# Transposing the late attention chunks by DMA, with a new load order at the start, in a retention-plus-FFN kernel

## Chip, cores, metric

The kernel runs on one core of a Trainium2 chip (trn2). The metric is device time in microseconds (us) of one execution; the quoted times are medians of repeated executions, and the profile is one further execution.

## The reference, cut to what matters

```python
# q, k, v: (B=4, H=8, S=768, D=64), fp32
for t in range(S):
    state = gamma * state + outer(k[t], v[t])        # one 64x64 state per head
    y[t] = scale * (q[t] @ state)
x = y.transpose(0, 2, 1, 3).reshape(3072, 512)
h = maximum(x @ w_in, 0)                             # w_in 512 x 2048   ("FFN1")
out = (h * h) @ w_out                                # w_out 2048 x 512  ("FFN2")
```

The kernel cuts the sequence into 24 chunks of 128 tokens with all eight heads. A chunk's attention is a *visit* on TensorE: scores and state sums of one chunk, and values and state application of the chunk before. It needs k and q with the head dimension on the partitions, that is transposed; this transposition is what the change is about. Each chunk then passes FFN1 and FFN2.

## The kernel before

The kernel is a list of operations with estimated durations. A small list scheduler in the program places them and so fixes the instruction order of every engine and of the DMA issues on SyncE's queue (SP). The hardware then runs each engine's list in order, waiting on semaphores. The estimates don't make the kernel fast or slow by themselves, but they decide what stands behind what.

```python
SMALL = (1.20, 1.55, 65)      # a 256 KB load of one chunk's k, q or v: 256-byte runs
PAIR  = (1.4, 1.6, 9)         # a 512 KB load of k or q of two chunks: long runs
BLOCKS = [1, 1, 2, 2, 2, 4, 4, 4, 4]     # chunks of one FFN1 pass
LEAD = 7                      # attention visits this many chunks ahead of the FFN
ORDER = "p0 i0 i1 p1 i2 i3 o0 o1 o2 p2 o3"   # p: pair of chunks, i: quarter of w_in, o: of w_out
...
    def flips(m):             # transposition in the visit: 32 TensorE transposes of 64x64
        for x, name in enumerate("kq"):
            for j in range(NJ):
                for sub in range(2):
                    r = slice(L * sub, L * sub + L)
                    for a in range(2):
                        nc.tensor.transpose(tpv[...], bf[name][m % NBF][r, j, a, :], ident[r, r])
    def evacuate(m):          # PSUM -> SBUF on ScalarE
        pl.add(f"E{m}", "ACT", 1.0, ("yy0", "yy1"), qkeys(m), lambda: nc.scalar.activation(...))
...
        def fn():             # one visit
            if t is not None: flips(t)
            if m is not None: values(m); apply(m, 0); ...
            if n is not None: scores(n); sums(n)
            if m is not None: ...; apply(m, 1)
```

The first six chunks are loaded in pairs and transposed by another TensorE routine (`flip_rows`, left out here), the other 18 by `flips`, one chunk ahead.

Of the kernel before, what the change touches and what calls it, by code (L numbers as in the profile page):

```python
# [18 lines left out]
class Plan:  # L19
# [44 lines left out]
    def schedule(self, nbanks, max_open):  # L64
# [21 lines left out]
        shared = [0.0, 0.0]  # L86
# [3 lines left out]
        while done < n:  # L90
# [25 lines left out]
            if move:  # L116
                out_ = outstanding[eng]
                while out_ and out_[0][0] <= t:
                    out_.pop(0)
                while sum(x[1] for x in out_) + dur[2] > self.RING:  # L120
                    t = max(t, out_.pop(0)[0])
# [8 lines left out]
            if move:  # L130
                dur, n_desc = (dur[:2] if t < 50 else dur[:1] * 2), dur[2]
                eng_free[eng] = t + 0.08
                for w in range(2):
                    shared[w] = max(shared[w], t + self.DMA_LATENCY) + dur[w]
                end[i] = max(shared) + self.LAND
                out_.append((max(shared), n_desc))
                dur = 0.08
            else:
                if eng == "PE":
# [6 lines left out]
                    while issued + todo > edge:  # L146
# [7 lines left out]
                        next_fetched = ahead + min(5.7, max(0.3, max(shared) - ahead)) + self.FETCH  # L154
# [23 lines left out]
SMALL = (1.20, 1.55, 65)  # L178
PAIR = (1.4, 1.6, 9)
WIDE = (2.75, 2.75, 33)  # L180
STORE = (0.72, 0.72, 9)
BLOCKS = [1, 1, 2, 2, 2, 4, 4, 4, 4]
SPLIT = 6
WARM = 20.0
FILL = 0.8
PACE = 6
LEAD = 7
NFP = 3
F2LAG = 5.0
# [7 lines left out]
ORDER = "p0 i0 i1 p1 i2 i3 o0 o1 o2 p2 o3"  # L197


def dma_order(nm):  # L200

    seq = []
    for t in ORDER.split() + [f"c{m}" for m in range(nm)]:
        n = int(t[1:])
        if t[0] == "p":
            new = [("k", 2 * n), ("q", 2 * n), ("v", 2 * n), ("v", 2 * n + 1)]
        else:
            new = [(x, n) for x in "kqv"] if t[0] == "c" else [("in" if t[0] == "i" else "out", n)]
        seq += [x for x in new if x not in seq]
    return seq  # L210
# [3 lines left out]
def kernel(  # L214
# [32 lines left out]
    NLD, NBF, NQT, NXT, NH2, NWS, NOSB, NST = 4, 4, 4, 4, 3, 4, 3, 6  # L247
# [18 lines left out]
    bf = {x: [sb(f"{x}s{j}", [P, NJ, 2, D] if x != "v" else [P, H, D], BF16) for j in range(NBF)] for x in "qkv"}  # L266
# [81 lines left out]
    def prepare(m):  # L348
        b, i = where(m)
        slot = m % NLD  # L350
        for x in "kqv":
            t = ld[x][:, slot, :]
            if x != "v" and m < 2 * NFP:
                if m % 2 == 0:
                    pl.add(f"ld{x}{m}", "SP", PAIR, (), (f"ld{x}{slot}", f"ld{x}{slot + 1}"),
                           lambda x=x: nc.sync.dma_start(  # L356
                               ld[x][:, slot : slot + 2, :].rearrange("s u n -> s (u n)"),
                               src[x][b, :, i * C : (i + 2) * C, :].rearrange("h (w t) d -> w h (t d)", t=16)),
                           prio=dma_prio[(x, m)])
                continue  # L360
            pl.add(f"ld{x}{m}", "SP", SMALL, (), (f"ld{x}{slot}",),
                   lambda x=x, t=t: nc.sync.dma_start(  # L362
                       t.rearrange("s (h d) -> s h d", h=H),
                       src[x][b, :, i * C : (i + 1) * C, :].rearrange("h s d -> s h d")),
                   prio=dma_prio[(x, m)])
        for x in "kq":
            t, o = ld[x][:, slot, :], bf[x][m % NBF]
            if m < 2 * NFP:
                pl.add(f"c{x}{m}", CAST[x], 0, (f"ld{x}{slot}",), (f"bf{x}{m % NBF}",),
                       lambda on, t=t, o=o: copy_on(on, o.rearrange("s j a d -> s (j a d)"), t), prio=urgency(m))  # L370
                continue
# [8 lines left out]
               prio=urgency(m))  # L380

# [10 lines left out]
    def flip_rows(m, x):  # L392


        to, key = (sc, "sc") if x == "k" else (yy, "yy")
        for u in range(2):
            bt = bf[x][(m + u) % NBF].rearrange("s j a d -> s (j a d)")

            def fn(u=u, bt=bt):
                for t in range(8):  # L400
                    for a in range(2):
                        nc.tensor.matmul(to[L * a : L * a + L, u, L * t : L * t + L], lhsT=bt[:, t * D : t * D + D],  # L402
                                         rhs=ident.rearrange("p (w h) -> p w h", h=H)[:, :, NJ * a : NJ * a + NJ],
                                         start=True, stop=True, skip_group_check=True)
            pl.add(f"T{x}{m}.{u}", "PE", 0.35, (f"bf{x}{(m + u) % NBF}", "ident"), (f"{key}{u}",), fn,
                   prio=-200 + m, lat=0.2, count=16)
        cols = to.rearrange("p s n -> p (s n)").rearrange("p (t u w j) -> p u j w t", u=2, j=NJ, w=8)
        for u in range(2):
            o = qkts[(m + u) % NQT][:, "kq".index(x)].rearrange("p j (w t) -> p j w t", t=16)
            pl.add(f"E{x}{m + u}", EVAC, 0, (f"{key}0", f"{key}1"), (f"qkT{(m + u) % NQT}.{x}",),  # L410
                   lambda on, u=u, o=o: copy_on(on, o, cols[:, u]), prio=urgency(m + u), lat=0.05)

    def natural_keys(m):

# [15 lines left out]
    def qkeys(m):  # L430
        return [f"qkT{m % NQT}.{x}" for x in "kq"]
# [295 lines left out]
```

## Time and profile before

| | before |
|---|---|
| median | 226.32 us (225.99 to 226.65, 3 runs) |
| profiled span | 225.5 us |
| TensorE (PE) busy | 204.8 us, 91% |
| all FFN at full rate | 24 x 8 x 0.865 = 166 us (four 128x512 matmuls take 0.865 us) |

The table of windows of the kernel before follows. Its columns are: stretch in us and its length; busy us (with instruction count) of PE, PEld (weight loads), VectorE (DVE), ScalarE (ACT), GpSimd (POOL); granted TensorE clock (1.00 is full speed); DMA share (mean busy share of the 16 DMA engines; it can pass 1, because packets overlap and each is counted where it starts); GB/s.

```profile
24.00:30.00 6.00, 4.41 (x145) 3.90 (x143) 5.54 (x12) 3.86 (x8) 1.36 (x3) 1.00 1.03 364
36.00:42.00 6.00, 3.44 (x59) 2.87 (x57) 3.39 (x8) 2.61 (x6) 1.64 (x2) 1.00 1.05 190
42.00:48.00 6.00, 5.52 (x102) 4.12 (x102) 5.33 (x12) 3.55 (x7) 0.88 (x2) 1.00 0.94 300
48.00:60.00 12.00, 11.71 (x213) 5.80 (x215) 4.25 (x8) 5.01 (x8) 4.91 (x8) 1.00 1.03 245
96.00:108.00 12.00, 11.89 (x312) 6.27 (x315) 11.74 (x25) 8.82 (x14) 3.65 (x6) 1.00 0.89 193
```

Before 48 us DMA is full (share about 1) and PE has gaps; after it PE is nearly full. Weights move at some 360 GB/s, the small loads at 190 to 200. A second view is the chain of waits of before, start and length in us: TensorE's progress hangs on DMA until 42 us, above all on the queries of the third pair.

```profile
10.01 6.26 SPq L362
16.31 5.24 SPq L569
25.69 16.56 DMA qn<-in_q_dram
42.37 0.81 POOL qs L345
```

The third view is the timeline of TensorE in one visit of before: start, length, line, tiles. L389 is `flips`.

```profile
98.38 0.32 PE L389 MATMUL yy<-ident,ks 64*64 64x64 bf16 x16
98.53 0.30 PE L389 MATMUL yy<-ident,qs 64*64 64x64 bf16 x16
98.65 0.30 PE L453 MATMUL yy<-pt,vs 64*64 64x64 bf16 x16
98.78 0.24 PE L468 MATMUL yy<-qkT,state 64*64 64x64 bf16 x8
98.84 0.31 PE L479 MATMUL sc<-qkT 64*64 64x64 bf16 x16
98.97 0.32 PE L490 MATMUL sc<-vs,ks 64*64 64x64 bf16 x16
99.11 0.27 PE L468 MATMUL yy<-qkT,state 64*64 64x64 bf16 x8
99.31 0.39 PE L593 MATMUL fps<-xt,w_in 128*128 128x512 bf16 x1
```

Matmuls are pipelined, so one reads from start to start: the flips hold TensorE from 98.38 to 98.65, 0.27 us, of a visit of 0.93 us.

### The profile page before, as it was taken

How to read it: one execution, taken by the hardware profiler on the slowest of the kernel's cores; microseconds unless marked ns; L12 is line 12 of the kernel's file. 1: busy time of each engine (PE TensorE's matmuls, PEld its weight loads, DVE VectorE, ACT ScalarE, POOL GpSimd, SP SyncE). 2: the span in 40 equal slices, each digit the busy share in tenths (PEclk: the TensorE clock that was granted, in tenths of full speed). 3: DMA queues.
4: the chain of work that ended last, by engine and by line, in shares of the span. 5: the costliest groups of instructions: out<-in, count | busy, mean ns of one | idle time of the engine just before them, and what ended most of it. 6: DMA issues, size and time to landing. Idle time of an engine off the chain costs nothing.

```text
span 225.5 us, 7244 instructions
## 1 busy us (share of the span) xinstructions
PE 204.8 (91%) x3210; PEld 116.0 (51%) x3236; DVE 112.7 (50%) x250; ACT 106.0 (47%) x168; POOL 39.0 (17%) x65
## 2 busy tenths in 40 slices
PE   4786778699999999999989999999999999999993
PEld 1545667554577875455545554444444444444441
DVE  1583955873188786699957765432222222220000
ACT  8315635644357552677555555434335444343121
POOL 3213224224323322332242200000000000000000
PEclk9997999999999999999999999999999999999999
DMA  6999999999999999998988510110011110111212
GB/s 150 265 337 189 337 376 237 184 346 197 283 211 200 236 187 213 231 202 179 206 188 177 146 49 3 47 49 12 35 47 47 49 47 1 47 49 47 93 49 91
DMA packets 70975, 34.02 MB, mean 151 GB/s; under 512 B 63008, under 2 KB 63008, under 8 KB 70944
## 3 DMA queue, kind: packets, MB, share of 16 engines
q1 hardware_dynamic: 70944, 33.56, 58.8%
q8 instruction: 25, 0.41, 0.8%
q14 instruction: 6, 0.05, 0.1%
HBM read 27.26 MB, written 6.29 MB: 149 GB/s over the span
## 4 chain that ended last, share of the span: by engine, by line
PE 75%; SPq 11%; DMA 7%; issue 2%; ACT 2%; DVE 1%; POOL 0%; ACTq 0%; POOLq 0%
PE fps L631 34%; PE fps L593 32%; DMA qn<-in_q_dram 7%; SPq L569 6%; SPq L362 4%; PE yy L389 3%; PE yy L468 2%; SPq L356 2%; PE yy L453 1%; ACT qkT L436 1%; PE sc L479 1%; PE sc L490 1%; DVE xt L555 1%; POOL qs L345 0%; PE yy L402 0%
## 5 line engine op out<-in xcount | busy, mean ns | idle before, releaser
L593 PE MATMUL fps<-xt,w_in 128*128 128x512 bf16 (+2 forms) x566 | 93.7, 309 | 3.9 <-POOL w_in L345 2.0
L631 PE MATMUL fps<-w_out,h 128*128 128x512 bf16 x368 | 90.1, 379 | 1.7 <-issue 1.3
L598 ACT ACTIVATE h<-fps 128x512 bf16<-128x512 f32 x96 | 56.6, 596 | 52.6 <-PE fps L593 51.5
L593 PEld LDWEIGHTS <-w_in 128*128 128x128 bf16 x576 | 50.5, 99 | 35.4 <-issue 2.1
L603 DVE TENSOR_TENSOR h<-h 128x512 bf16<-128x512 bf16 x96 | 42.4, 456 | 49.7 <-ACT h L598 49.5
L631 PEld LDWEIGHTS <-h 128*128 128x128 bf16 x384 | 36.7, 98 | 42.9
L555 DVE TENSOR_TENSOR xt<-yy,yf 128x512 bf16<-128x512 f32 x24 | 16.6, 690 | 21.6 <-ACT qkT L436 18.1
L436 ACT ACTIVATE qkT<-yy 128x1024 bf16<-128x1024 bf16 x18 | 18.4, 1023 | 18.2 <-PE yy L468 17.5
L639 ACT ACTIVATE osb<-fps 128x512 f32<-128x512 f32 x24 | 14.3, 597 | 21.7 <-PE fps L631 21.4
L377 DVE TENSOR_TENSOR vs<-vn,vf 128x512 bf16<-128x512 f32 x24 | 17.6, 735 | 4.8 <-DMA vn<-in_v_dram 4.8
L345 POOL CAST ks<-kn 128x512 bf16<-128x512 f32 x20 | 13.5, 677 | 35.0 <-DMA kn<-in_k_dram 19.8
L345 POOL CAST qs<-qn 128x512 bf16<-128x512 f32 x21 | 14.7, 701 | 27.3 <-DMA qn<-in_q_dram 27.3
L546 DVE TENSOR_TENSOR state<-sc,state 128x256 bf16<-128x256 f32 x40 | 16.7, 419 | 0.5
L533 DVE TENSOR_TENSOR pt<-sc,cmask 128x512 bf16<-128x512 f32 x24 | 16.3, 681 | 0.0
L468 PE MATMUL yy<-qkT,state 64*64 64x64 bf16 x352 | 12.5, 198 | 1.0 <-issue 0.6
L453 PE MATMUL yy<-pt,vs 64*64 64x64 bf16 x384 | 7.8, 195 | 2.8 <-DVE pt L533 1.4
L468 PEld LDWEIGHTS <-state 64*64 64x64 bf16 x352 | 7.6, 105 | 2.0 <-PE yy L468 1.1
L453 PEld LDWEIGHTS <-vs 64*64 64x64 bf16 x384 | 5.3, 107 | 5.5 <-issue 2.9
L479 PE MATMUL sc<-qkT 64*64 64x64 bf16 x384 | 7.9, 196 | 0.1
L341 ACT ACTIVATE w_in<-wst 128x512 bf16<-128x512 f32 x7 | 4.1, 623 | 7.7 <-DMA wst<-in_moe_w_in_dram 7.6
L490 PE MATMUL sc<-vs,ks 64*64 64x64 bf16 x352 | 7.6, 196 | 0.0
L693 PE MATMUL fps<-ident 128*128 128x512 bf16 x12 | 5.8, 605 | 1.6 <-POOL ident L297 1.6
(45 smaller groups left out, 85.0 us busy)
## 6 DMA issues: line engine op xcount, KB each, us to landing
vn<-in_v_dram SPq DMA_DIRECT2D x24, 256.0 KB, 5.9
out_dram<-osb SPq DMA_DIRECT2D x24, 256.0 KB, 2.0
kn<-in_k_dram SPq DMA_DIRECT2D x18, 256.0 KB, 5.5
qn<-in_q_dram SPq DMA_DIRECT2D x18, 256.0 KB, 5.7
wst<-in_moe_w_in_dram SPq DMA_DIRECT2D x4, 1024.0 KB, 9.7
wst<-in_moe_w_out_dram SPq DMA_DIRECT2D x4, 1024.0 KB, 10.5
kn<-in_k_dram SPq DMA_DIRECT2D x3, 512.0 KB, 11.6
qn<-in_q_dram SPq DMA_DIRECT2D x3, 512.0 KB, 13.4
```

What stands on the lines that cost most here:

```text
L345: nc.gpsimd.tensor_copy(o, t)
L377: lambda: nc.vector.tensor_tensor(out=o[:], in0=t.rearrange("s (h d) -> s h d", h=H), in1=vf[:, i, :, None].to_broadcast([P, H, D]), op=AL ...
L436: lambda: nc.scalar.activation(qkT.rearrange("p x j (s t) -> p s (x j) t", s=2), tpv.rearrange("p s (g t) -> p s g t", t=L), AF.Copy), pri ...
L453: nc.tensor.matmul(yy[L * c : L * c + L, sub, p * L : p * L + L], lhsT=vs[r, 4 * a + j, :], rhs=pt[r, a, j, :], start=(p == 0), stop=True, ...
L468: nc.tensor.matmul(yy[L * c : L * c + L, sub, p * L : p * L + L], lhsT=st[r, j, :], rhs=qkT[r, 1, j, sub * L : sub * L + L], start=False, ...
L533: lambda: nc.vector.tensor_tensor(out=pt[:], in0=sc[:, :, 0:256].rearrange("s g (p t) -> s g p t", p=NJ), in1=cmask[:, None, None, :].to_b ...
L546: f = lambda cc=cc, j1=j1, j0=j0: nc.vector.tensor_tensor(out=sts[j1][:], in0=cc, in1=sts[j0][:], op=ALU.add)
L555: lambda: nc.vector.tensor_tensor(out=xt[:, :, u * C : u * C + C].rearrange("s p (g t) -> s g p t", g=2), in0=yy[:, :, 0:256].rearrange("s ...
L593: nc.tensor.matmul(ps[:, u * n : u * n + n], lhsT=w_in_bf[j][:, cb, c * P : (c + 1) * P], rhs=xt[:, cb, cols], start=(cb == 0), stop=(cb = ...
L598: nc.scalar.activation(h2[:, f0 : f0 + per, cols], ps[:].rearrange("p (u n) -> p u n", u=per), AF.Relu)
L603: nc.vector.tensor_mul(hv, hv, hv)
L631: nc.tensor.matmul(ps[:], lhsT=h2[:, fb, u * C : u * C + C], rhs=w_out_bf[j][:, c, :], start=(fb == 0), stop=(fb == NFB - 1))
```

## The change

The intent: from the ninth chunk on, let the DMA transpose k and q, four chunks ahead, so that TensorE and ScalarE are rid of it; and at the start fetch four chunks before the weights, so that their attention is done while TensorE would be idle. Single-chunk loads replace the pairs; the first four queries are issued on ScalarE's queue; FFN1 starts with six single chunks; the last chunk's FFN2 is cut into two halves.

```diff
-BLOCKS = [1, 1, 2, 2, 2, 4, 4, 4, 4]
+BLOCKS = [1, 1, 1, 1, 1, 1, 2, 2, 2, 4, 4, 4]
+AHEAD = 4
-LEAD = 7
+LEAD = 2
+NPE = 6      # chunks 0-5: eight 128x128 TensorE transposes each, outside the visit
+NTD = 8      # chunks 6, 7: flips in the visit; from 8 on: DMA
+QACT = 4
-F2LAG = 5.0
+F2LAG = 3.0
-ORDER = "p0 i0 i1 p1 i2 i3 o0 o1 o2 p2 o3"
+ORDER = ("k0 q0 q1 v0 k1 q2 v1 k2 v2 v3 k3 q3 i0 i1 q4 o0 i2 i3 k4 o1 v4 o2 o3 v5 v6 q5 k5 q6 v7 q7 k6 k7")
...
+            side = x == "q" and m < QACT
+            pl.add(f"ld{x}{m}", "ACT" if side else "SP", SMALL, (), (f"ld{x}{slot}",), ...
...
+        if m >= NPE:
+            pl.add(f"X{m}", "SP", TURN, (f"bfk{m % NBF}", f"bfq{m % NBF}"), qkeys(m),
+                   lambda: nc.sync.dma_start_transpose(out=qkT..., in_=t...), prio=-0.5)
...
+            parts = 2 if q4 == NM - 1 else 1      # FFN2 of the last chunk in halves
+                    ... prio=(q4 + F2LAG) * 8 + 2 * j + 1 + part * 0.5
```

(`flip_rows` and its helpers go; buffers of the bf16 and transposed k/q grow from 4 to 5; the scheduler's model of DMA is simplified and its estimates for DMAs are changed; PACE, the number of first visits that go ahead of everything else, grows from 6 to 8.)

More of the change, by code (lines that the diff above doesn't have):

```diff
@@ L85, in schedule @@
         open_groups = set()
-        shared = [0.0, 0.0]
+        pipe = 0.0
         outstanding = {e: [] for e in eng_free}
@@ L116, in schedule @@
             if move:
+                cost, n_desc, hold = dur
                 out_ = outstanding[eng]
@@ L119, in schedule @@
                     out_.pop(0)
-                while sum(x[1] for x in out_) + dur[2] > self.RING:
+                while sum(x[1] for x in out_) + n_desc > self.RING:
                     t = max(t, out_.pop(0)[0])
@@ L130, in schedule @@
             if move:
-                dur, n_desc = (dur[:2] if t < 50 else dur[:1] * 2), dur[2]
-                eng_free[eng] = t + 0.08
-                for w in range(2):
-                    shared[w] = max(shared[w], t + self.DMA_LATENCY) + dur[w]
-                end[i] = max(shared) + self.LAND
-                out_.append((max(shared), n_desc))
-                dur = 0.08
+                eng_free[eng] = t + hold
+                pipe = max(pipe, t + self.DMA_LATENCY) + cost
+                end[i] = pipe + self.LAND
+                out_.append((pipe, n_desc))
+                dur = hold
             else:
@@ L153, in schedule @@
                         edge += self.BLOCK
-                        next_fetched = ahead + min(5.7, max(0.3, max(shared) - ahead)) + self.FETCH
+                        next_fetched = ahead + min(5.7, max(0.3, pipe - ahead)) + self.FETCH
                     issued += todo
@@ L175, in schedule @@
         return sorted(range(n), key=lambda i: (start[i], i))
-SMALL = (1.20, 1.55, 65)
-PAIR = (1.4, 1.6, 9)
-WIDE = (2.75, 2.75, 33)
-STORE = (0.72, 0.72, 9)
-BLOCKS = [1, 1, 2, 2, 2, 4, 4, 4, 4]
+SMALL = (1.20, 65, 0.6)
+TURN = (1.10, 16, 2.4)
+WIDE = (2.85, 33, 0.6)
+STORE = (0.80, 9, 0.6)
+BLOCKS = [1, 1, 1, 1, 1, 1, 2, 2, 2, 4, 4, 4]
 SPLIT = 6
+AHEAD = 4
 WARM = 20.0
 FILL = 0.8
-PACE = 6
-LEAD = 7
-NFP = 3
-F2LAG = 5.0
+PACE = 8
+LEAD = 2
[3 more added lines that the diff above has]
+F2LAG = 3.0
 F2WAIT = 4
@@ L194 @@
 WPRIO = {"in": -2.0, "out": 2.0}
-ORDER = "p0 i0 i1 p1 i2 i3 o0 o1 o2 p2 o3"
+ORDER = (
+    "k0 q0 q1 v0 k1 q2 v1 k2 v2 v3 k3 q3 i0 i1 q4 o0 i2 i3 k4 o1 v4 o2 o3 v5 v6 q5 k5 q6 v7 q7 k6 k7"
+)
 def dma_order(nm):
-    seq = []
-    for t in ORDER.split() + [f"c{m}" for m in range(nm)]:
-        n = int(t[1:])
-        if t[0] == "p":
-            new = [("k", 2 * n), ("q", 2 * n), ("v", 2 * n), ("v", 2 * n + 1)]
-        else:
-            new = [(x, n) for x in "kqv"] if t[0] == "c" else [("in" if t[0] == "i" else "out", n)]
-        seq += [x for x in new if x not in seq]
-    return seq
+    names = {"i": "in", "o": "out"}
+    seq = [(names.get(t[0], t[0]), int(t[1:])) for t in ORDER.split()]
+    return seq + [(x, m) for m in range(nm) for x in "kqv" if (x, m) not in seq]
 @with_exitstack
@@ L246 @@
         assert 512 % (n * C) == 0 and x // 4 == (x + n - 1) // 4
-    NLD, NBF, NQT, NXT, NH2, NWS, NOSB, NST = 4, 4, 4, 4, 3, 4, 3, 6
+    NLD, NBF, NQT, NXT, NH2, NWS, NOSB, NST = 4, 5, 5, 4, 3, 4, 3, 6
     NBANK = 4
@@ L265 @@
     ld = {x: sb(f"{x}n", [P, NLD, H * D], FP32) for x in "qkv"}
-    bf = {x: [sb(f"{x}s{j}", [P, NJ, 2, D] if x != "v" else [P, H, D], BF16) for j in range(NBF)] for x in "qkv"}
+    kq = [sb(f"kqs{j}", [P, 2, NJ, 2, D], BF16) for j in range(NBF)]
+    bf = {"k": [t[:, 0] for t in kq], "q": [t[:, 1] for t in kq]}
+    bf["v"] = [sb(f"vs{j}", [P, H, D], BF16) for j in range(NBF)]
     qkts = [sb(f"qkT{j}", [P, 2, NJ, P], BF16) for j in range(NQT)]
@@ L352, in prepare @@
             t = ld[x][:, slot, :]
-            if x != "v" and m < 2 * NFP:
-                if m % 2 == 0:
-                    pl.add(f"ld{x}{m}", "SP", PAIR, (), (f"ld{x}{slot}", f"ld{x}{slot + 1}"),
-                           lambda x=x: nc.sync.dma_start(
-                               ld[x][:, slot : slot + 2, :].rearrange("s u n -> s (u n)"),
-                               src[x][b, :, i * C : (i + 2) * C, :].rearrange("h (w t) d -> w h (t d)", t=16)),
-                           prio=dma_prio[(x, m)])
-                continue
-            pl.add(f"ld{x}{m}", "SP", SMALL, (), (f"ld{x}{slot}",),
-                   lambda x=x, t=t: nc.sync.dma_start(
+            side = x == "q" and m < QACT
+            pl.add(f"ld{x}{m}", "ACT" if side else "SP", SMALL, (), (f"ld{x}{slot}",),
+                   lambda x=x, t=t, q_=nc.scalar if side else nc.sync: q_.dma_start(
                        t.rearrange("s (h d) -> s h d", h=H),
                        src[x][b, :, i * C : (i + 1) * C, :].rearrange("h s d -> s h d")),
-                   prio=dma_prio[(x, m)])
+                   prio=dma_prio[(x, m)] - 200 * side)
         for x in "kq":
             t, o = ld[x][:, slot, :], bf[x][m % NBF]
-            if m < 2 * NFP:
-                pl.add(f"c{x}{m}", CAST[x], 0, (f"ld{x}{slot}",), (f"bf{x}{m % NBF}",),
-                       lambda on, t=t, o=o: copy_on(on, o.rearrange("s j a d -> s (j a d)"), t), prio=urgency(m))
-                continue
             pl.add(f"c{x}{m}", CAST[x], 0, (f"ld{x}{slot}",), (f"bf{x}{m % NBF}",),
@@ L380, in prepare, with qkeys @@
                prio=urgency(m))
+    def qkeys(m):
+        return [f"qkT{m % NQT}.{x}" for x in "kq"]
     def flips(m):
@@ L390, in flips @@
                                             bf[name][m % NBF][r, j, a, :], ident[r, r])
-    def flip_rows(m, x):
-        to, key = (sc, "sc") if x == "k" else (yy, "yy")
-        for u in range(2):
-            bt = bf[x][(m + u) % NBF].rearrange("s j a d -> s (j a d)")
-            def fn(u=u, bt=bt):
-                for t in range(8):
-                    for a in range(2):
-                        nc.tensor.matmul(to[L * a : L * a + L, u, L * t : L * t + L], lhsT=bt[:, t * D : t * D + D],
-                                         rhs=ident.rearrange("p (w h) -> p w h", h=H)[:, :, NJ * a : NJ * a + NJ],
-                                         start=True, stop=True, skip_group_check=True)
-            pl.add(f"T{x}{m}.{u}", "PE", 0.35, (f"bf{x}{(m + u) % NBF}", "ident"), (f"{key}{u}",), fn,
-                   prio=-200 + m, lat=0.2, count=16)
-        cols = to.rearrange("p s n -> p (s n)").rearrange("p (t u w j) -> p u j w t", u=2, j=NJ, w=8)
-        for u in range(2):
-            o = qkts[(m + u) % NQT][:, "kq".index(x)].rearrange("p j (w t) -> p j w t", t=16)
-            pl.add(f"E{x}{m + u}", EVAC, 0, (f"{key}0", f"{key}1"), (f"qkT{(m + u) % NQT}.{x}",),
-                   lambda on, u=u, o=o: copy_on(on, o, cols[:, u]), prio=urgency(m + u), lat=0.05)
-    def natural_keys(m):
-        qkT, ks = qkts[m % NQT], bf["k"][m % NBF]
-        o1 = {}
-        def back():
-            ps = fps[o1["op"]["bank_index"]].bitcast(BF16)
-            for j in range(NJ):
-                nc.tensor.transpose(ps[:, j * P : j * P + P], qkT[:, 0, j, :], ident[:])
-        i0 = pl.add(f"B{m}", "PE", 0.24, (qkeys(m)[0], "ident"), (f"gB{m}",), back, prio=-200 + m, lat=0.2, count=4,
-                    bank=("open", ("B", m), False))
-        o1["op"] = pl.ops[i0]
-        pl.add(f"G{m}", EVAC, 0, (f"gB{m}",), (f"bfk{m % NBF}",),
-               lambda on: copy_on(on, ks.rearrange("s j a d -> s (j a d)"),
-                                  fps[o1["op"]["bank_index"]].bitcast(BF16)[:, 0:512]),
-               prio=urgency(m), bank=("close", ("B", m)))
-    def qkeys(m):
-        return [f"qkT{m % NQT}.{x}" for x in "kq"]
     def evacuate(m):
@@ L440, in transpose, with fn @@
     def transpose(m):
-        pl.add(f"T{m}", "PE", 0.45, (f"bfk{m % NBF}", f"bfq{m % NBF}", "ident"), ("yy0", "yy1"),
-               lambda: flips(m), prio=-200 + m, lat=0.2, count=32)
-        evacuate(m)
+        qkT, t = qkts[m % NQT], kq[m % NBF]
+        if NPE <= m < NTD:
+            return
+        if m >= NPE:
+            pl.add(f"X{m}", "SP", TURN, (f"bfk{m % NBF}", f"bfq{m % NBF}"), qkeys(m),
+                   lambda: nc.sync.dma_start_transpose(out=qkT.rearrange("p x j t -> p (x j) t"),
+                                                       in_=t.rearrange("s x j a d -> s (x j a d)")), prio=-0.5)
+            return
+        for x, name in enumerate("kq"):
+            o1 = {}
+            def fn(x=x, o1=o1):
+                ps = fps[o1["op"]["bank_index"]].bitcast(BF16)
+                for j in range(NJ):
+                    nc.tensor.transpose(ps[:, j * P : j * P + P], t[:, x, j].rearrange("s a d -> s (a d)"), ident[:])
+            i0 = pl.add(f"T{name}{m}", "PE", 0.26, (f"bf{name}{m % NBF}", "ident"), (f"gT{name}{m}",), fn,
+                        prio=-200 + m, lat=0.2, count=4, bank=("open", ("T", m, x), False))
+            o1["op"] = pl.ops[i0]
+            pl.add(f"E{name}{m}", EVAC, 0, (f"gT{name}{m}",), (qkeys(m)[x],),
+                   lambda on, x=x, o1=o1: copy_on(on, qkT[:, x].rearrange("p j t -> p (j t)"),
+                                                  fps[o1["op"]["bank_index"]].bitcast(BF16)[:, 0:512]),
+                   prio=urgency(m), lat=0.05, bank=("close", ("T", m, x)))
     def values(m):
@@ L521, in fn @@
                 apply(m, 1)
-        dur = 0.19 + (0.26 if m is not None else 0) + (0.26 if n is not None else 0) + (0.26 if t is not None else 0)
+        dur = 0.19 + 0.26 * ((m is not None) + (n is not None) + (t is not None))
         if n is None:
@@ L620, in ffn2 @@
             h2 = h2s[g % NH2]
-            grp = ("f2", q4)
-            o1 = {}
             slot = q4 % NOSB
-            for j in range(4):
-                reads = [f"h{g % NH2}.{u}.{4 * j + c}" for c in range(4)] + [f"wout{j}.{c}" for c in range(4)]
-                def mm(j=j, o1=o1, h2=h2, u=u):
-                    ps = fps[o1["op"]["bank_index"]]
-                    for c in range(4):
-                        fb = 4 * j + c
-                        nc.tensor.matmul(ps[:], lhsT=h2[:, fb, u * C : u * C + C], rhs=w_out_bf[j][:, c, :],
-                                         start=(fb == 0), stop=(fb == NFB - 1))
-                i0 = pl.add(f"F2.{q4}.{j}", "PE", 0.866, reads, (f"g{grp}",), mm,
-                            prio=(q4 + F2LAG) * 8 + 2 * j + 1, lat=0.2,
-                            bank=("open", grp, True) if j == 0 else ("use", grp), count=4)
-                if j == 0:
-                    o1["op"] = pl.ops[i0]
@@ L638, in ffn2 @@
-            pl.add(f"O{q4}", "ACT", 0.6, (f"g{grp}",), (f"osb{slot}",),
-                   lambda o1=o1, slot=slot: nc.scalar.activation(
-                       osbs[slot][:], fps[o1["op"]["bank_index"]][:], AF.Copy),
-                   prio=q4, bank=("close", grp))
-            pl.add(f"st{q4}", "SP", STORE, (f"osb{slot}",), (),
-                   lambda q4=q4, slot=slot: nc.sync.dma_start(out[rows(q4) : rows(q4) + C, :], osbs[slot][:]), prio=-1)
+            parts = 2 if q4 == NM - 1 else 1
@@ new lines, in ffn2, with mm @@
+            w = DM // parts
+            for part in range(parts):
+                ns = slice(part * w, part * w + w)
+                grp = ("f2", q4, part)
+                keys = [f"osb{slot}.{part}"] if parts > 1 else [f"osb{slot}.0", f"osb{slot}.1"]
+                o1 = {}
+                for j in range(4):
+                    reads = [f"h{g % NH2}.{u}.{4 * j + c}" for c in range(4)] + [f"wout{j}.{c}" for c in range(4)]
+                    def mm(j=j, o1=o1, h2=h2, u=u, ns=ns, w=w):
+                        ps = fps[o1["op"]["bank_index"]]
+                        for c in range(4):
+                            fb = 4 * j + c
+                            nc.tensor.matmul(ps[:, 0:w], lhsT=h2[:, fb, u * C : u * C + C], rhs=w_out_bf[j][:, c, ns],
+                                             start=(fb == 0), stop=(fb == NFB - 1))
+                    i0 = pl.add(f"F2.{q4}.{j}" + f"/{part}" * (parts > 1), "PE", 0.866 / parts, reads, (f"g{grp}",), mm,
+                                prio=(q4 + F2LAG) * 8 + 2 * j + 1 + part * 0.5, lat=0.2,
+                                bank=("open", grp, True) if j == 0 else ("use", grp), count=4)
+                    if j == 0:
+                        o1["op"] = pl.ops[i0]
+                pl.add(f"O{q4}" + f"/{part}" * (parts > 1), "ACT", 0.2 + 0.4 / parts, (f"g{grp}",), keys,
+                       lambda o1=o1, slot=slot, ns=ns, w=w: nc.scalar.activation(
+                           osbs[slot][:, ns], fps[o1["op"]["bank_index"]][:, 0:w], AF.Copy),
+                       prio=q4, bank=("close", grp))
+                pl.add(f"st{q4}" + f"/{part}" * (parts > 1), "SP", STORE, keys, (),
+                       lambda q4=q4, slot=slot, ns=ns: nc.sync.dma_start(out[rows(q4) : rows(q4) + C, ns], osbs[slot][:, ns]),
+                       prio=-1)
@@ L653 @@
         n = m + 1
-        early = n < 2 * NFP and n % 2 == 0
-        if early:
-            prepare(n)
-            prepare(n + 1)
-            flip_rows(n, "k")
-        elif 2 * NFP <= n <= SPLIT:
-            prepare(n)
-        if n < NM and n < SPLIT:
+        for x in range(0 if m < 0 else m + AHEAD, min(NM, m + AHEAD + 1)):
+            prepare(x)
+            transpose(x)
+        t = m + 2 if NPE <= m + 2 < NTD else None
+        if n < SPLIT:
             if m >= 0:
                 visit(m, None)
-            if early:
-                flip_rows(n, "q")
-                natural_keys(n)
-                natural_keys(n + 1)
-            elif n >= 2 * NFP:
-                transpose(n)
-            visit(None, n)
-        else:
-            if n == SPLIT:
-                transpose(n)
-            t = n + 1 if n + 1 < NM else None
-            if t is not None:
-                prepare(t)
-            visit(m if m >= 0 else None, n if n < NM else None, t)
+            visit(None, n, t)
+        else:
+            visit(m, n if n < NM else None, t)
         while done < NB and blk0[done] + blocks[done] - 1 == m:
```

## The prediction

> **What bounds the kernel now.** From 48 us to the end TensorE: in the table of windows PE is busy about 11.3 to 11.95 of every 12 us, and 66% of the chain of waits are the FFN matmuls (L593, L631). Before 48 us input DMA: its share is about 1.0 in nearly every window, and the chain consists of DMA issues, waits for weights, and one 16.6 us wait for the third query pair (25.7 to 42.3 us). In the TensorE timeline only four chunks of FFN1 and 11 of 16 matmuls of one chunk of FFN2 are done by 49 us: 16.6 us of FFN. Four 128x512 matmuls take 0.865 us, so all FFN costs 24 x 8 x 0.865 = 166 us.
>
> **What changes, costed.**
>
> 1. *16 of 18 in-loop flips leave TensorE.* In the timeline, start to start, the 32 small transposes L389 take 0.28 us of a visit; the rest takes about 0.65. All lie in the TensorE-bound part: 16 x 0.28 = 4.5 us, critical. Their ScalarE evacuations (L436, 1.02 us) go too, off the path.
> 2. *DMA transposes replace them*, 256 KB each. The Trainium skill (Advanced Engine Details and Errata, X-Bar Transpose (TRN2)) gives 350 to 400 GB/s; I estimate 0.65 to 0.75 us of DMA each. This trace has none. A chunk's three loads (256-byte packets, about 200 GB/s) take 1.3 us each; with transpose and store 5.5 us against 7.5 of TensorE. Issued four chunks ahead, they should not hold TensorE up, even at two or three times the cost.
> 3. *Startup order.* Paired k/q loads (4 KB packets) become per-chunk loads, dearer for DMA, but chunks 0 to 3 come before the weights, so their attention is done while TensorE would idle. Weights run at about 390 GB/s, 2.7 us per MB. Up to the last weight: 15 small x 1.3 + 8 x 2.7 + 2 = 43 us (now: last w_out cast at 51). First w_in at about 21 us, all of w_in near 34. FFN1 of chunks 0 to 3 should end near 38, FFN2 of two chunks advance with each w_out, TensorE saturate near 43 to 47 with 21 to 22 us of FFN done by 49 us: gain about 5 us.
> 4. *Queries 0 to 3 on the ScalarE queue.* An SP issue takes 0.57 to 0.68 us; parallel issue feeds DMA earlier in the first 5 us. Gain 0.5 us.
> 5. *Six one-chunk blocks instead of two.* 32 matmuls of 128x128 take 1.96 us against 1.73 at full rate: +0.45 us a chunk, four more chunks, partly in the startup: +1.
> 6. *Last chunk in halves.* Last matmul to end is now 3.7 us (0.60 copy, then store). Gain 0.4.
>
> **Sum.** 226.3 - 4.5 - 5 - 0.5 - 0.4 + 1, plus 0.5 for hiccups with attention only two chunks ahead: about 217 us.
>
> **Predicted: 217.0 us, range 212 to 223. Faster by over 2% (below 221.8): 0.76; within 2%: 0.17; slower: 0.07.**
>
> **What would show it.** L389 falls from 576 to 64 matmuls, L436 from 18 to 2; steady visits shrink by 0.28 us; the TensorE-bound stretch starts before 48 us; the last w_out lands near 43 us and no query wait of over 10 us stands in the chain; DMA transposes land within about 10 us and no TensorE wait names them; TensorE stays above 95% busy from 48 us on.
>
> **What would make it wrong.** Transposes that occupy DMA or SP's issue far longer and hold up loads behind them in the in-order queue; small loads filling slower than 200 GB/s in the startup; visits two chunks ahead exposing VectorE's 0.7 us steps (it is 98% busy between 96 and 108 us).

## The result

| | before | after |
|---|---|---|
| median, timed together | 226.49 us (225.99 to 227.6, 4 runs) | 217.76 us (217.31 to 218.69, 4 runs) |
| profiled span | 225.5 us | 216.9 us |
| PE busy | 204.8 us | 203.6 us |
| FFN matmul done by 49 us | 16.4 us | 21.6 us |
| FFN matmul done by 60 us | 25.1 us | 31.6 us |
| last matmul to end of span | 3.8 us | 3.6 us |

The ratio is 0.9614, 95% interval 0.9564 to 0.9663. A ratio here is the mean time of one kernel's fast runs over that of the other's of the same rounds, so it is not quite the ratio of the medians quoted. FFN done is worked out from the weight loads of the two FFN lines in the table of windows: a 128-column matmul counted as 0.054 us, 256 columns as 0.108, 512 columns as 0.216 (0.865 / 4), whatever it really took.

The windows of the kernel after, and the chain at its start:

```profile
24.00:30.00 6.00, 5.92 (x99) 5.72 (x100) 3.58 (x8) 3.15 (x6) 2.19 (x3) 1.00 1.08 359
36.00:42.00 6.00, 5.94 (x137) 5.02 (x134) 5.38 (x13) 3.65 (x8) 2.10 (x3) 1.00 1.09 355
42.00:48.00 6.00, 5.98 (x66) 4.06 (x67) 4.62 (x11) 2.60 (x5) 1.15 (x3) 1.00 1.03 240
48.00:60.00 12.00, 12.00 (x135) 6.56 (x133) 3.58 (x8) 4.01 (x6) 4.47 (x8) 1.00 0.96 213
84.00:96.00 12.00, 10.48 (x185) 7.28 (x184) 7.80 (x17) 4.27 (x8) 3.46 (x5) 1.00 1.46 191
96.00:108.00 12.00, 11.74 (x192) 8.02 (x191) 7.48 (x15) 4.49 (x8) 2.58 (x4) 1.00 1.19 209
```

```profile
13.51 7.65 DMA wst<-in_moe_w_in_dram
21.88 2.07 PE fps L565 x16
24.82 4.30 PE fps L565 x48
29.34 6.25 PE fps L565 x112
```

From 22 us on TensorE has work, where before it stood idle for a quarter of the time from 24 to 48 us. The wait of 16.6 us is gone. But there is a dent that was not there before: 10.48 of 12 us between 84 and 96. The waits of TensorE after 48 us name it (total us, times, longest):

```profile
PE sc L451 <- DMA qkT<-kqs: 2.7, 3, 1.5
```

and the timeline of a visit after, with no flips, runs from 105.47 to 106.14, 0.67 us:

```profile
105.47 0.32 PE L425 MATMUL yy<-pt,vs 64*64 64x64 bf16 x16
105.62 0.23 PE L440 MATMUL yy<-qkT,state 64*64 64x64 bf16 x8
105.68 0.30 PE L451 MATMUL sc<-qkT 64*64 64x64 bf16 x16
105.81 0.31 PE L462 MATMUL sc<-vs,kqs 64*64 64x64 bf16 x16
105.94 0.27 PE L440 MATMUL yy<-qkT,state 64*64 64x64 bf16 x8
106.14 0.39 PE L608 MATMUL fps<-w_out,h 128*128 128x512 bf16 x1
```

The page's list of DMA issues after has the new kind (median us from issue to landing last):

```profile
qkT<-kqs SPq DMA_TRANSPOSE x16, 5.6
```

**The 8.6 us of the two spans, split at 60 us.** By 60 us, 6.5 us more FFN is done. After 60 us the spans have 165.5 and 156.9 us left, of which 140.9 and 134.4 are FFN; so the rest fell only from 24.6 to 22.5 us, by 2.1. In that rest I can name 15 flips fewer (16 before, 1 after; 15 x 0.27 = 4.0 us); against it one visit more to do (by 60 us seven chunks had their scores before, six after; 0.67), about as much waiting (2.7 us for transposes in place of 2.5 us of other waits), and 0.2 us for a sixth chunk in 128-column matmuls (its two runs of 32 take 1.87 and 1.79 us from start to start, against 1.73 at full rate); the tail is 0.2 us shorter. That leaves 3.1 against the 2.1 found: about 1 us of the rest I cannot name.

The total was predicted almost to the microsecond. The terms were not, and the experiments ask about each.

### The profile page after: what moved, and what is told of

The parts are those of the page before. It is cut to its first block, busy times and chain, and to the rows that moved or that the text cites. A ratio compares the mean times of both kernels' runs of the same rounds, so it can differ in the third digit from the quotient of the medians.

```text
span 216.9 us, 6314 instructions
## 1 busy us (share of the span) xinstructions
PE 203.6 (94%) x2765; PEld 121.6 (56%) x2765; DVE 111.6 (51%) x250; ACT 86.5 (40%) x144; POOL 39.8 (18%) x68
## 4 chain that ended last, share of the span: by engine, by line
PE 77%; DMA 13%; SPq 5%; DVE 1%; issue 1%; ACT 1%; POOL 0%; ACTq 0%
PE fps L608 36%; PE fps L565 34%; DMA qkT<-kqs 8%; SPq L355 4%; DMA wst<-in_moe_w_in_dram 4%; DMA qn<-in_q_dram 2%; PE yy L425 2%; PE yy L440 2%; PE sc L451 1%; PE sc L462 1%; DVE xt L527 1%; ACT qkT L387 0%; PE fps L408 0%; SPq L620 0%; PE yy L381 0%
## 5 line engine op out<-in xcount | busy, mean ns | idle before, releaser
L565 PE MATMUL fps<-xt,w_in 128*128 128x128 bf16 (+2 forms) x768 | 95.4, 278 | 0.8 <-POOL w_in L345 0.8
L608 PE MATMUL fps<-w_out,h 128*128 128x512 bf16 (+1 forms) x400 | 92.6, 371 | 0.0
L565 PEld LDWEIGHTS <-w_in 128*128 128x128 bf16 x768 | 61.4, 101 | 30.1 <-POOL w_in L345 0.9
L616 ACT ACTIVATE osb<-fps 128x512 f32<-128x512 f32 (+1 forms) x25 | 14.4, 580 | 31.9 <-PE fps L608 31.9
L345 POOL CAST kqs<-kn 128x512 bf16<-128x512 f32 x23 | 14.7, 639 | 66.4 <-DMA kn<-in_k_dram 54.2
L345 POOL CAST kqs<-qn 128x512 bf16<-128x512 f32 x24 | 16.2, 675 | 23.4 <-DMA qn<-in_q_dram 21.6
L505 DVE TENSOR_TENSOR pt<-sc,cmask 128x512 bf16<-128x512 f32 x24 | 16.4, 681 | 6.3 <-PE sc L462 6.3
L408 PE MATMUL fps<-ident,kqs 128*128 128x128 bf16 x48 | 6.5, 279 | 4.1 <-POOL kqs L345 4.1
L657 PE MATMUL fps<-ident 128*128 128x512 bf16 x13 | 7.1, 626 | 1.6 <-POOL ident L297 1.6
L408 PEld LDWEIGHTS <-kqs 128*128 128x128 bf16 x48 | 4.2, 121 | 7.9 <-POOL kqs L345 6.8
L451 PEld LDWEIGHTS <-qkT 64*64 64x64 bf16 x384 | 5.6, 114 | 4.4 <-DMA qkT<-kqs 3.0
```

Of the source, the lines that this page charges most:

```text
L345: nc.gpsimd.tensor_copy(o, t)
L451: nc.tensor.matmul(sc[cs, a, j * L : j * L + L], lhsT=qkT[r, 0, j, cs], rhs=qkT[r, 1, j, cs], start=(j == 0), stop=True, skip_group_check= ...
L505: lambda: nc.vector.tensor_tensor(out=pt[:], in0=sc[:, :, 0:256].rearrange("s g (p t) -> s g p t", p=NJ), in1=cmask[:, None, None, :].to_b ...
L565: nc.tensor.matmul(ps[:, u * n : u * n + n], lhsT=w_in_bf[j][:, cb, c * P : (c + 1) * P], rhs=xt[:, cb, cols], start=(cb == 0), stop=(cb = ...
L608: nc.tensor.matmul(ps[:, 0:w], lhsT=h2[:, fb, u * C : u * C + C], rhs=w_out_bf[j][:, c, ns], start=(fb == 0), stop=(fb == NFB - 1))
```

## The experiments

Twelve kernels ran, four at a time on one chip together with the kernel before. "Ratio" is to the kernel before. All results were correct. The three calls ran on different chips, where the kernel before took 226.57, 226.04 and 226.17 us; a difference between medians of two calls is uncertain by about that much. The first call had after_again, flips_all, order_old and q_on_sp, the second blocks_old, lead_old, xpose_twice and ahead5, the third the rest.

| run | what | median us | ratio (95%) |
|---|---|---|---|
| after_again | the change, unedited | 217.62 | 0.9637 (0.9595 to 0.9679) |
| flips_all | no DMA transposes | 221.26 | 0.9794 (0.9742 to 0.9847) |
| order_old | old load order, no ScalarE issue | 223.21 | 0.9882 (0.9837 to 0.9928) |
| q_on_sp | no ScalarE issue | 216.11 | 0.9569 (0.9523 to 0.9615) |
| blocks_old | old FFN1 blocks | 220.94 (5 runs) | 0.9768 (0.9727 to 0.9808) |
| lead_old | old LEAD and F2LAG | 217.33 | 0.9623 (0.9588 to 0.9658) |
| xpose_twice | each DMA transpose twice | 231.35 | 1.0237 (1.0189 to 1.0286) |
| ahead5 | five chunks ahead | 217.57 | 0.9628 (0.9590 to 0.9666) |
| best | q_on_sp, last halves in turn | 215.46 | 0.9544 (0.9502 to 0.9586) |
| copy_beside | a plain copy beside each transpose | 229.87 | 1.0186 (1.0140 to 1.0231) |
| before_early | before, with early pairs and single blocks | 229.15 | 1.0147 (1.0093 to 1.0201) |
| blocks_old2 | blocks_old, one look | 220.61 | (one run, state unknown) |

FFN done, from the windows of each profile, in us of matmul:

| | before | after_again | flips_all | order_old | q_on_sp | blocks_old2 | before_early |
|---|---|---|---|---|---|---|---|
| by 49 us | 16.4 | 21.8 | 22.1 | 19.0 | 22.7 | 21.6 | 13.8 |
| by 60 us | 25.1 | 31.8 | 31.8 | 25.7 | 32.0 | 27.7 | 22.9 |

### The yardstick

> Control: the changed kernel unedited, as the yardstick for the runs beside it. Every theory expects 217 to 219 us, a ratio to the kernel before of about 0.962.

217.62 us (216.95 to 218.6, 6 runs): the result repeats.

### Are the DMA transposes worth anything?

```diff
-NTD = 8
+NTD = 24
```

> All chunks from the seventh on are transposed on TensorE inside the visits again, no DMA transposes; all else as changed. My theory: 16 flips x 0.28 us come back (+4.5 us), the three TensorE waits for a DMA transpose (2.7 us in the profile of after) go, so a net +2 to +3 us: 219.5 to 221 us; no DMA_TRANSPOSE, no DMA wait on TensorE after 48 us. Rival A, the DMA transposes gave nothing net and the whole gain is the startup: 217 to 218.5 us. Rival B, the flips cost more than their own TensorE time (their evacuation on ScalarE and the shared PSUM banks held up the visits): 222 us or more.

Measured 221.26 us, 3.6 above the unedited change, just over the top of my range and under Rival B's. The startup is untouched (the same FFN by 60 us), so Rival A falls: the transposes are worth 3.6 us, less than the 16 x 0.27 = 4.3 us of TensorE time that they free. TensorE's waits for qkT (2.0 us in the yardstick's profile) are gone; one of 0.9 us for VectorE's xt is new.

### Is it the load order?

```diff
-"k0 q0 q1 v0 k1 q2 v1 k2 v2 v3 k3 q3 i0 i1 q4 o0 i2 i3 k4 o1 v4 o2 o3 v5 v6 q5 k5 q6 v7 q7 k6 k7"
+"k0 k1 q0 q1 v0 v1 i0 i1 k2 k3 q2 q3 v2 v3 i2 i3 o0 o1 o2 k4 k5 q4 q5 v4 v5 o3"
-QACT = 4
+QACT = 0
```

> The loads are issued in the order of the kernel before (chunks 0 and 1, two quarters of w_in, chunks 2 and 3, the rest of the weights between), all on the SP queue; small loads, one-chunk blocks, DMA transposes stay. My theory, that about 5 us of the gain come from having four chunks ready before the weights so that TensorE saturates at 43 to 47 us: 221 to 223 us, with FFN done by 49 us back near 17 us of matmul. Rival, that the order matters little and the finer blocks and earlier FFN2 made the startup gain: 217.5 to 219 us.

223.21 us, as my theory had it (just above its range), though FFN by 49 us fell only to 19.0 us and not to the 17 it named. The fair neighbour is q_on_sp, which has the queries on SP too: 7.1 us between them. The table shows where: 25.7 us of FFN by 60 us against 32.0, which is 6.3 of the 7.1. The windows of 48 to 60 us, order_old first and then q_on_sp, show TensorE waiting in one and not in the other:

```profile
48.00:60.00 12.00, 9.20 (x268) 7.06 (x262) 6.88 (x14) 6.11 (x9) 4.14 (x6) 1.00 1.05 235
```

```profile
48.00:60.00 12.00, 11.79 (x151) 6.28 (x154) 4.31 (x8) 4.17 (x7) 5.04 (x8) 1.00 1.11 245
```

So the order is the largest single part of the change, larger than the 5 us I gave the whole startup.

### Queries on ScalarE's queue

```diff
-QACT = 4
+QACT = 0
```

> The first four query loads are issued on SP again. My theory: only issue time is saved, and DMA is the bound for the first 40 us, so 0 to +0.5 us: 217.8 to 218.3 us. Rival, that the early parallel issue matters because the first weights start later in an in-order queue: +1 us or more, with the first w_in landing over 1 us later than at 21 us.

Neither theory: 216.11 us, *faster* than the change by 1.5 us (no run of the one overlaps a run of the other: 215.26 to 216.75 against 216.95 to 218.6). The timeline shows what I had not asked about. The issues hold ScalarE itself. The kernel after:

```profile
0.73 5.52 ACTq L355 DMA_DIRECT2D qn<-in_q_dram  x4
6.28 1.28 ACT L330 ACT_TABLE_LOAD   x1 [6.28 <-issue]
7.58 0.24 ACT L330 ACTIVATE vf<-ex_f 128x48 f32<-128x48 f32 x1
7.85 0.19 DVE L332 TENSOR_SCALAR vf<-vf 128x48 f32<-128x48 f32 x1 [5.71 <-ACT vf L330]
```

and q_on_sp:

```profile
0.73 1.28 ACT L330 ACT_TABLE_LOAD   x1 [0.73 <-PEq L675]
2.03 0.24 ACT L330 ACTIVATE vf<-ex_f 128x48 f32<-128x48 f32 x1
2.30 0.19 DVE L332 TENSOR_SCALAR vf<-vf 128x48 f32<-128x48 f32 x1 [0.15 <-ACT vf L330]
```

In the change ScalarE is busy issuing from 0.73 to 6.25 us, so the decay factors vf, which scale every v, come 5.5 us later and VectorE waits 5.7 us for them. The Trainium skill (DMA: Bandwidth & Descriptors, section Issuing engines are not separate DMA queues) says that issuing from several engines at once "will only save the time on the sequencer it takes to initiate the DMA". The case agrees that no bandwidth is won (218 GB/s from 6 to 12 us in both), and adds that the second queue's engine pays: four issues took 5.52 us, 1.4 each, against 0.46 us for SP's first. Nor was DMA fed earlier: by 6 us it had moved 0.90 MB in the change and 0.93 MB in q_on_sp, and SP's own issues in the first 8 us took up to 2.35 us beside ScalarE's, against at most 1.25 without them. That the lost 1.5 us come from ScalarE's delay is not shown, and the profiles speak against it for the most part: by 49 us q_on_sp has 0.9 us more FFN done, but by 60 us only 0.2, with as many visits (six), while the two spans differ by 2.5 us. Most of the gain comes after 60 us. There the waits for transposes fell from 2.0 to 0.3 us, and the scheduler had laid out another order throughout.

### FFN1 in single chunks

```diff
-BLOCKS = [1, 1, 1, 1, 1, 1, 2, 2, 2, 4, 4, 4]
+BLOCKS = [1, 1, 2, 2, 2, 4, 4, 4, 4]
```

> FFN1 blocks of 1, 1, 2, 2, 2, 4, 4, 4, 4 chunks as before instead of six single ones; all else as changed. My prediction counted the single blocks as a cost of 1 us (128-column matmuls at 61 ns against 54). If that is all they do: 216.5 to 217.5 us. Rival, that single chunks let FFN1 start on each chunk as soon as it is there and so fill the startup: 219 us or more, with less FFN done by 49 us than the 22 us of the changed kernel.

220.94 us: the single blocks gain 3.3 us (3.0 by the two ratios); I had counted them as a loss of 1. One of the six runs, the profiled one, took 347 us at a granted clock of 0.575; it is left out. Its second look:

> The old FFN1 blocks once more, for a profile: the first one ran at a granted clock of 0.575 and shows nothing. Timed runs were 221.0 us, 3.4 above the changed kernel. If the single blocks fill the startup: by 49 us less FFN is done than the 22 us of the changed kernel, by about 3 us. If they act later (the pace of visits and transposes): about 22 us by 49 us, and new waits after 49 us.

220.61 us. By 49 us 21.6 us of FFN are done, as much as in the change, by 60 us only 27.7 against 31.8. So it is the second branch, "they act later": FFN1 of chunks 4 and 5 as one block cannot begin until the later of them has arrived and been visited. TensorE, timeline of blocks_old2:

```profile
57.31 0.45 PE L381 MATMUL yy<-ident,kqs 64*64 64x64 bf16 x32 [1.12 <-POOL kqs L345]
58.05 0.27 PE L440 MATMUL yy<-qkT,state 64*64 64x64 bf16 x8
60.20 2.13 PE L565 MATMUL fps<-xt,w_in 128*128 128x256 bf16 x10 [1.89 <-DVE xt L527]
```

A block of two waits for its second member just when FFN2's backlog has run out: PE is busy 9.19 of the 12 us from 48 to 60. After the gap the granted clock read 0.86 from 60 to 72 us; what that adds to the loss was not separated.

### Two chunks ahead or seven

```diff
-LEAD = 2
-F2LAG = 3.0
+LEAD = 7
+F2LAG = 5.0
```

> Attention visits seven chunks ahead and FFN2 lag 5 as before, instead of two and 3. If visits two chunks ahead expose waits (I allowed 0.5 us): 217 us. If being close to the FFN is what gives the DMA transposes time to land: TensorE meets transposes that have not landed much more often, since it now asks for each chunk earlier: over 220 us, with over 5 us of TensorE waits for qkT.

217.33 us, no difference from the change that the spread would show; the TensorE waits for qkT are 1.9 us, no more. Both theories overrated it. My "0.5 us for hiccups" has nothing to stand on, and the closeness of the visits is not what lets the transposes land.

### Where do the waits for transposes come from?

```diff
-NBF, NQT, NXT = 5, 5, 4
+NBF, NQT, NXT = 6, 6, 3
-AHEAD = 4
+AHEAD = 5
```

> Loads, casts and transposes five chunks ahead instead of four (one more buffer of each; one xt buffer fewer to make room). If the three TensorE waits for transposes (2.0 to 2.7 us in the two profiles) are lack of lead: they go, 215 to 216 us. If they come from the SP's order, each transpose holding up the loads behind it, so that the pace and not the lead is short: the waits stay at 1.5 us or more, 217 to 218.5 us.

217.57 us and 1.9 us of waits in four pieces: more lead does not remove them (with one xt buffer fewer, whose own effect was not tested). That speaks for the pace of the in-order SP queue, not for too short a lead, but shows it only by exclusion. A transpose stands on SP behind the loads of its own chunk and ahead of the next chunk's; SP waits at transposes for a cast (10.9 us in all in the kernel after):

```profile
SPq L399 <- POOL kqs L345: 10.9, 6, 3.6
```

### What does one transpose cost the DMA?

```diff
+            pl.add(f"XX{m}", "SP", TURN, (f"bfk{m % NBF}", f"bfq{m % NBF}"), ("spare",),
+                   lambda: nc.sync.dma_start_transpose(out=spare..., in_=t...), prio=-0.4)
```

> Each DMA transpose is issued a second time into a spare tile; the result stays right. Theory from the packets of the changed kernel: a transpose first holds all 16 engines 1 to 2 us and then moves 1,024 packets of 256 bytes, so 2 to 3 us of DMA each, and SP holds 1.4 us or more to issue; then a chunk needs some 10 us of DMA against 7.5 of TensorE, and TensorE waits for qkT or loads: +15 us or more, 232 us and up. If a transpose costs 0.7 us of DMA, as I estimated from the Trainium skill, a chunk needs 6.3 us and nothing but a few more waits follows: below 221 us.

231.35 us, 13.7 more than the change. Taken alone this would have "confirmed" that a transpose is dear. The control replaced the second transpose by a copy:

```diff
-                   lambda: nc.sync.dma_start_transpose(out=spare..., in_=t...), prio=-0.4)
+                   lambda: nc.sync.dma_start(spare..., t...), prio=-0.4)
```

> As the doubled transposes, but the second DMA is a plain copy of the same 256 KB between the same tiles, not a transpose. If the 13.7 us that the doubled transposes cost come from transposing (the engines held 1 to 2 us before the 256-byte packets, and SP's 1.3 us): a plain copy, one row per partition, costs 0.7 us of DMA and 0.5 us of SP, and TensorE hardly waits more: below 220.5 us. If any 256 KB more in this stretch costs the same: 228 us or more.

229.87 us: a plain copy costs nearly as much, so my reading of xpose_twice falls. Nor is it bandwidth. The windows of copy_beside around its largest stall:

```profile
108.00:112.00 4.00, 4.00 (x81) 2.67 (x79) 2.66 (x7) 2.37 (x4) 0.00 (x0) 1.00 0.33 93
120.00:124.00 4.00, 0.00 (x0) 0.00 (x0) 0.69 (x1) 0.00 (x0) 1.23 (x2) 0.77 1.15 238
```

DMA had time to spare from 108 to 112 us (share 0.33), and TensorE then starved from 120 to 124. SP's waits between 106 and 122 us, and TensorE's between 100 and 140:

```profile
SPq L624 <- ACT osb L620: 6.2, 3, 4.1
```

```profile
PE sc L455 <- DMA qkT<-kqs: 5.1, 1, 5.1
```

SP stood for 6.2 us at *stores* of output blocks that TensorE had not yet computed; the transpose that TensorE needed next was behind them in the queue, issued at 120.33 us, 0.7 us after the last of those stores. Both added DMAs have the same place and the same estimate in the scheduler (2.4 us of SP, 1.1 us of DMA), so both give the same layout of the SP queue, and at this stall it is the layout that costs; how much of the other loss is layout, and how much the added 256 KB and SP's issue time, was not separated. Part of the loss is the clock: in both profiles the granted clock reads 1.00 from 116 to 120 us and 0.50 to 0.52 in each window of 4 us from 124 to 136 us, after the stall. The difference of the two runs, 1.5 us, is between two calls, and the intervals of their ratios overlap; it is no measure of the price of a transpose.

That price can be read where a transpose runs alone. In copy_beside the last transpose is issued at 180.32 us, with DMA idle just before its packets (0 GB/s from 181.0 to 181.5); it holds SP for 1.25 us and lands after 3.1 us. The last plain copy of the same 256 KB, issued at 186.92 us beside a store, holds SP for 0.48 us and lands after 2.5 us. Windows of half a us, transpose first:

```profile
182.00:182.50 0.50, 0.50 (x4) 0.26 (x3) 0.35 (x1) 0.12 (x1) 0.00 (x0) 1.00 1.14 205
187.50:188.00 0.50, 0.50 (x4) 0.20 (x2) 0.00 (x0) 0.39 (x1) 0.00 (x0) 1.00 1.03 385
```

At 205 GB/s the 256 KB of a transpose take 1.3 us of DMA, at 385 GB/s those of a copy 0.7 (both worked out from these rates).

In the unedited kernel the last transpose, issued at 149.60 us with nothing behind it, looks worse:

```profile
152.50:153.00 0.50, 0.50 (x4) 0.21 (x3) 0.09 (x1) 0.50 (x1) 0.00 (x0) 1.00 0.67 4
153.00:153.50 0.50, 0.50 (x5) 0.20 (x3) 0.42 (x1) 0.24 (x1) 0.00 (x0) 1.00 0.02 2
153.50:154.00 0.50, 0.50 (x4) 0.27 (x3) 0.00 (x0) 0.36 (x1) 0.00 (x0) 1.00 0.08 9
154.50:155.00 0.50, 0.50 (x4) 0.20 (x2) 0.43 (x1) 0.23 (x2) 0.00 (x0) 1.00 0.61 131
```

For 1.5 us hardly a packet starts, with PE and the other engines going on, and then a last 128 KB, half of the transpose, moves at some 130 GB/s. (The window before, 152.0 to 152.5, reads a DMA share of 5.93: packets begun there were still open during the stop.) But this stop is not the transpose's own. In q_on_sp the last transpose is issued at 152.23 us, four us after the last load, and runs through without one:

```profile
153.50:154.00 0.50, 0.50 (x4) 0.21 (x3) 0.26 (x1) 0.17 (x1) 0.00 (x0) 1.00 1.08 210
```

It lands after 3.0 us. In the unedited kernel a load of v was issued 0.9 us ahead of the transpose, and an instruction fetch of 16 KB falls in the stop; whether one of them makes it stays open. A transpose alone thus takes nearly twice the 0.7 us I estimated, and beside other traffic it can take longer (up to 6.1 us from issue to landing), but TensorE seldom sees it.

### The startup idea on the old loads

```diff
 # in the kernel before
-BLOCKS = [1, 1, 2, 2, 2, 4, 4, 4, 4]
+BLOCKS = [1, 1, 1, 1, 1, 1, 2, 2, 2, 4, 4, 4]
-ORDER = "p0 i0 i1 p1 i2 i3 o0 o1 o2 p2 o3"
+ORDER = "p0 p1 i0 i1 o0 i2 i3 o1 p2 o2 o3"
```

> The kernel before with nothing but the new startup idea: both first pairs (chunks 0 to 3) loaded ahead of all weights, and six single FFN1 blocks; paired loads, flips, visits seven ahead stay. If order and blocks are the startup gain: 226 less 4 to 6, so 220 to 222 us. If they need the per-chunk loads (a pair delivers its first chunk only when both have landed): 224 us or more.

229.15 us, 3 *slower* than before: inside the second range (224 us or more), but neither theory had it slower than before. By 49 us only 13.8 us of FFN are done, no FFN2 at all: the scheduler did not keep the order I asked for and put the third pair ahead of all of w_out (first w_out issued at 27.8 us, 23.6 before). So this run is not a clean test of paired against single loads. It shows that "four chunks first" and single blocks do not carry over as two constants; whether the pairs themselves are at fault stays open.

### The best version tried

```diff
-QACT = 4
+QACT = 0
-prio=(q4 + F2LAG) * 8 + 2 * j + 1 + part * 0.5
+prio=(q4 + F2LAG) * 8 + 2 * j + 1 + part * 8
```

> The changed kernel with the first four queries back on SP, and the last chunk's two FFN2 halves done one after the other, not interleaved. The queries alone gave 216.1 us beside 217.6. In the changed kernel both halves are evacuated after the last matmul, 3.6 us from it to the end as before the change; done in turn, the first half is stored while the second is computed, so the tail should shrink to about 3.3 us and the time be 215.5 to 216.2 us. If the tail is only the store's latency whatever its size: no change, 216.1 us.

215.46 us, the fastest of all, at 0.9544 of before. Beside q_on_sp (0.9569) the difference is inside the intervals. The tail is not what helped: from the last matmul to the end it is 4.1 us here, 4.0 in q_on_sp, 3.6 in the change, 3.8 before. The first half is stored early, but the end still waits for the second half's store: 3.7 us from the end of its copy, against 3.1 for the whole chunk before. My expectation of 3.3 us was wrong.

## Why the prediction was right or wrong, point by point

Predicted 217.0, measured 217.76, inside the range. What the sum predicted as 4.5 us net in the startup (5 + 0.5 - 1) and 4.4 later (4.5 + 0.4 - 0.5) came as 6.5 and 2.1. Errors of opposite sign cancelled: that the total came so close was luck.

1. **Flips leave TensorE: the mechanism was right, the net too large.** The visit shrank by 0.26 us (0.93 to 0.67), as forecast. Taking the DMA transposes back out costs 3.6 us, not 4.5: part is given back in waits for transposes, of which I had said that none would be named (2.7 us in three).
2. **DMA transposes: harmless was nearly right, the price was not.** They land in 5.6 us (predicted within 10). My 0.65 to 0.75 us of DMA, from the 350 to 400 GB/s of the Trainium skill (Advanced Engine Details and Errata, X-Bar Transpose (TRN2)), is contradicted by the transposes that run alone: 205 to 210 GB/s, about 1.3 us each. The prediction survived because it allowed two to three times the cost.
3. **Startup order: right mechanism, too small.** FFN by 49 us was forecast at 21 to 22 and is 21.6; TensorE is full from about 24 us, earlier than the 43 to 47 I gave. But the gain is read at 60 us, not at 49: 6.5 us, and the old order alone costs 7.1. Between 49 and 60 us the kernel before does only 8.7 us of FFN, the changed one 10.0.
4. **Queries on ScalarE's queue: wrong sign.** Predicted gain 0.5; taking it out gains 1.5. The step that failed is "parallel issue feeds DMA earlier": DMA had moved no more by 6 us (0.90 against 0.93 MB), and ScalarE, whose time I left out, could not start its table load for 5.5 us. What the 1.5 us themselves are made of stays open: most of them show after 60 us.
5. **Single FFN1 blocks: wrong sign.** Predicted cost 1; they gain 3.3. I costed the matmul shape (61 against 54 ns; from start to start it is 56 to 58) and not the wait for the second chunk of a block.
6. **Last chunk in halves: little or nothing.** Predicted gain 0.4; the tail went from 3.8 to 3.6 us in one profile each, and it differs more than that among profiles with the same halves (3.2 us in flips_all, 4.0 in q_on_sp). The two halves are interleaved and end together; done in turn they leave it at 4.1.
7. **Visits two chunks ahead: nothing** (lead_old is equal); I had allowed 0.5.

The single effects of undoing (3.6 flips, 7.1 order, 3.3 blocks, -1.5 queries) sum to 12.5, more than the 8.7 us of the change (226.49 to 217.76). Order and blocks both show in the same gap at 48 to 60 us, so they probably overlap, and the single loads, the scheduler's changed estimates and PACE are undone in none of these runs. What they cost or gain was not measured.

## What to carry to other kernels

When several small changes come in one package, a right total says little about its terms: undo them one by one on the chip before keeping them all; here one of them cost 1.5 us. A DMA issued from a computing engine takes that engine's time: here four held ScalarE for 5.5 us at the start, ahead of the factors that every v needs. And in an in-order DMA queue, look at what stands ahead of the transfer: a store that waits for an engine that waits for a load behind it starves both, with DMA idle.

## What the Trainium skill lacked or had wrong

- DMA: Bandwidth & Descriptors (Issuing engines are not separate DMA queues): right that nothing is won in bandwidth (218 GB/s from 6 to 12 us with and without the second queue). It does not say how long a computing engine is held when it issues beside SP: four 256 KB loads held ScalarE for 5.52 us, SP's issues beside them took up to 2.35 us in place of 1.25, and the kernel with these loads on SP is 1.5 us faster.
- Advanced Engine Details and Errata (X-Bar Transpose (TRN2)): "TRN2 transpose DMAs are as fast as regular DMAs" was not seen here. A 256 KB transpose from SBUF to SBUF that ran alone moved at 205 to 210 GB/s, a plain copy of the same tile at 385 (beside a store); SP's issue took 1.25 us against 0.48. Beside other traffic landing took 4.6 to 6.1 us over the 16 of the change, and in one of them hardly a packet started for 1.5 us, a stop that the lone ones do not have. The DMA share then is no measure of work: it read 1.46 at 191 GB/s between 84 and 96 us.
- Perfetto Trace Analysis (DMA Optimizations) advises one issuing engine for inputs and another for outputs, but neither it nor another page gives this reason, the in-order trap between stores and loads on one issuing queue, or its size: with 16 DMAs added, SP waited 6.2 us at stores and TensorE 5.1 us for a transpose behind them, at a DMA share of 0.33.
